# A chunked RWKV-6 recurrence with a SiLU feed-forward: first weight loads moved in the DMA queue, the first two units' values multiplied straight into the rows of x, and first keys moved between engines

## The chip, the cores and the metric

The kernel runs on one core of one Trainium2 chip. The metric is the time of one execution on the device in microseconds (us). The profile is taken by the hardware profiler on one execution. Engines are named as in the profile: PE is TensorE (matrix multiply), PEld its weight load, DVE is VectorE, ACT is ScalarE, POOL is GpSimd, SP is SyncE, which here only issues DMA transfers, one after another in the order in which they are written.

## The reference

The kernel computes a recurrence over 768 tokens for 4 sequences and 8 heads of 48 channels, lays its output out as rows of 384 channels, and sends 3072 such rows through a feed-forward layer with a SiLU.

```python
# r, k, v, w: (4, 8, 768, 48); u: (8, 48)
for t in range(S):
    cur = np.einsum('bhd,bhe->bhde', u[None] * kt, vt)
    y[:, :, t] = np.einsum('bhd,bhde->bhe', rt, state + cur)
    state = wt[:, :, :, None] * state + np.einsum('bhd,bhe->bhde', kt, vt)
x = y.transpose(0, 2, 1, 3).reshape(B * S, H * D)      # 3072 x 384
h = x @ w_in                                            # 384 x 2048
g = h * (1.0 / (1.0 + np.exp(-h)))
return g @ w_out                                        # 2048 x 384
```

Everything is float32.

## The kernel before

**Units.** The work is cut into 12 units, numbered 0 to 11. A unit is 128 tokens of two sequences (b = 0, 1), so 256 rows of x. Two units cover a stretch of 128 tokens, and there are six stretches.

**The recurrence of a unit.** Instead of a loop over tokens the kernel makes a 128 x 128 matrix of scores for each sequence and head, in seven levels (block sizes 1, 2, 4 ... 64). `turn` brings r, k and w into a layout with channels on partitions (`tr`, `tk`, `tw`): for units 0 and 1 by matmuls with the identity (`turn_in`, `turn_out`), for later ones by a DVE transpose. `start_keys`, `grow_keys` and `grow_queries` multiply the keys and queries by products of w (`product`) level by level, `odd_keys` and `odd_ones` copy half of the keys on ACT, `scores` multiplies queries by keys on PE and copies the result into `score` under a mask on DVE. `bonus`, `bonus_sum`, `bonus_spread` and `bonus_write` make the diagonal, the term with u. For units 2 and 3 its numbers go through four small DMAs (`diag`) and five small ACT copies. `turn_apart` and `turn_k` bring the keys back for `update`, which makes the new state.

**From scores to x.** In units 0 and 1 the state is zero, so the output is scores times values. `y` (L872) does that for two heads at a time, in 64 partitions each with 48 used, and copies it to `yt` on ACT. `dense_x` (L910) multiplies `yt` by a 0/1 matrix `dense`, built at the start by `clear_dense` and `make_dense`, which packs the 8 x 48 channels into 3 x 128 partitions, and copies the result to `xt`. From unit 2 on, `y_state` and `y_values` make `yt` and `move_x` (L920) packs it into `xt` by ten DMAs on SP.

**Feed-forward.** `up(i, m)` (L995) multiplies 256 columns of w_in by `xt` (two blocks of 128 hidden channels, each over three blocks of 128 channels of x: 12 PE instructions) and applies the SiLU on ACT. `down` (unit 0) or `quarter` (seven products per unit on sums and differences, `sums` and `weight_sums` on DVE) multiplies by w_out.

**Weights.** Each of 16 blocks of weights (0 to 7 of w_in, 8 to 15 of w_out, 768 KB each) is loaded, split on ACT (`head_weight`, two instructions; `tail_weight`, one, into a PSUM room `p_w` of which there is one), joined on DVE (`join_weight`, two instructions) and added on POOL (`add_weight`). A block's load goes to one of seven places, and `join_weight(i)` issues the load of the block that takes over its place: 6 after 0, 7 after 1, 8 after 2, 9 after 3, 10 after 4, 11 after 5, 12 after 8, 13 after 9, 14 after 10, 15 after 11.

**Order.** Nothing is scheduled by a planner. The order of each engine's instructions is the order in which the steps are written in the `do(...)` lines (L1107 to L1163), and from unit 3 on the order that `mix(i)` gives. All of SP's transfers go through one queue: the blocks of r, k and w of a coming unit (`load_blocks`, 16 transfers for each of the three, of 32 and 16 KB), values (`load_values`, 5), tokens for the diagonal (`load_rk`), weights, diagonal, x and the outputs. A transfer that stands behind another is issued after it, even when what it needs is ready. The blocks of units 2, 3 and 4 are handed out by `block_loads` along the `do` lines; `mix(3)` hands out w and k of unit 5 (8 calls of 4 transfers each, with the values of unit 4 among them), and from `mix(4)` on also r of the next unit. `clear(0)` and `clear(1)` zero the unused half groups of `raw` on ACT once the first two units have been turned.

The line that decides which blocks `mix(i)` loads, in L981, and the steps it hands them to, L985:

```python
loads = [*at(i >= NPAIR and ahead, *block_loads(i + 1, "r")), *at(i + NSLOT < len(units), *block_loads(i + NSLOT, "wk"))]
behind = groups[10 if i < NPAIR else 5 if i == NPAIR else 2:][:4 if i + NSLOT >= len(units) else None]
```

NPAIR is 4 and NSLOT is 2. `move_x(i - 1)` stands in the second group of `mix(i)`, so after all that `mix(i - 1)` loads.

## Time and profile before

| | us |
|---|---|
| three runs | 598.10, 598.62, 599.99 |
| median | 598.62 |
| profiled execution, whole | 599.11 |
| its span, first to last instruction | 597.3 |
| PE busy in the span | 587.5 |
| POOL busy in the key products of L645, all units | 93.9 |
| six weight loads of w_in by SP, median from issue to landing | 7.6 |
| ten moves of x per unit, median from issue to landing of one | 1.9 |

The granted clock of PE is 1.000 throughout. In a timeline row the first number is the start in us from the start of the span, the second the duration, then engine, line, operation, what is written and what is read, and how many instructions the row merges; the brackets give the idle time of that engine just before and what ended it. In rows of SP's queue the duration of one transfer is its issue, not its movement.

### The profile page before, as it was taken

Reading aid. Unit: us, or ns where it says so; the run is one execution under the profiler, and the core shown is the slowest. Engines: PE = TensorE matmul, PEld = TensorE weight load, DVE = VectorE, ACT = ScalarE, POOL = GpSimd, SP = SyncE. Lnnn points to the kernel's source line nnn. Section 1 sums busy time; section 2 is a strip of 40 time slices with the busy share of each in tenths; the row PEclk is TensorE's granted clock in tenths of the full one; section 3 lists DMA queues with packets and bytes.
Section 4 is the critical chain, followed back from the end, with each engine's and each line's share of the span. In section 5 each row is a group of like instructions: output and inputs, shape, how many; then the busy total and the mean of one; then the engine's idle time right before and its main releaser. Section 6 shows DMA issues by size and latency. Waiting matters only on the chain.

```text
span 597.3 us, 14760 instructions
## 1 busy us (share of the span) xinstructions
PE 587.5 (98%) x5790; PEld 527.8 (88%) x5790; DVE 411.6 (69%) x709; ACT 232.7 (39%) x516; POOL 351.5 (59%) x414
## 2 busy tenths in 40 slices
PE   8999999999999999999999999999999999999997
PEld 7787866699899899899899899889889889889997
DVE  7879788798596695596696696686587587542041
ACT  6788874531530540440350351361351251250110
POOL 5998768447578568278378477477477567500000
PEclk9999999999999999999999999999999999999999
DMA  9965794443542543543543643643543531101000
GB/s 227 301 148 149 157 283 75 59 76 51 126 61 66 106 66 52 129 69 53 130 67 55 138 62 52 130 65 52 120 75 52 113 63 27 36 1 28 28 0 27
DMA packets 203078, 53.42 MB, mean 89 GB/s; under 512 B 186752, under 2 KB 194816, under 8 KB 203008
## 3 DMA queue, kind: packets, MB, share of 16 engines
q1 hardware_dynamic: 201424, 51.88, 42.7%
q8 instruction: 46, 0.75, 0.6%
q10 hardware_dynamic: 1584, 0.59, 0.5%
q14 instruction: 24, 0.20, 0.1%
HBM read 43.21 MB, written 5.24 MB: 81 GB/s over the span
## 4 chain that ended last, share of the span: by engine, by line
PE 82%; DVE 5%; POOL 4%; ACT 2%; SPq 2%; DMA 2%; issue 2%; POOLq 0%; DVEq 0%; ACTq 0%
PE p_h L1000 35%; PE p_o L1066 34%; PE p_m L1022 3%; PE p_m L864 2%; PE p_sc L703 2%; PE p_m L843 2%; SPq L123 2%; PE p_m L703 1%; DVE score L721 1%; POOL w_out_sb L255 1%; PE p_sc L892 1%; PE p_sc L819 1%; DMA own<-in_moe_w_out_dram 1%; DMA raw<-in_r_dram 1%; DVE score L604 1%
## 5 line engine op out<-in xcount | busy, mean ns | idle before, releaser
L1000 PE MATMUL p_h<-xt,w_in_sb 128*128 128x256 f32 x1152 | 259.8, 383 | 1.6 <-POOL tk L669 0.7
L1000 PEld LDWEIGHTS p_h<-xt,w_in_sb 128*128 128x128 f32 x1152 | 215.5, 190 | 33.3 <-ACT gt L1009 1.3
L1009 ACT ACTIVATE gt<-p_h 128x512 f32<-128x512 f32 x90 | 53.5, 595 | 172.5 <-PE p_h L1000 172.2
L645 POOL TENSOR_TENSOR tk<-tk,tw 128x256 f32<-128x256 f32 x128 | 93.9, 755 | 35.4 <-issue 21.0
L507 POOL TENSOR_TENSOR ruk<-tokens_rk 128x768 f32<-128x768 f32 (+1 forms) x32 | 51.4, 1616 | 64.4 <-DMA tokens_rk<-in_k_dram 34.6
L1066 PE MATMUL p_o<-own,temps 128*128 128x192 f32 x528 | 87.9, 326 | 0.0
L1066 PE MATMUL p_o<-w_out_sb,gt 128*128 128x192 f32 x508 | 86.4, 326 | 0.0
L1066 PEld LDWEIGHTS p_o<-own,temps 128*128 128x128 f32 x528 | 86.1, 190 | 0.1
L1066 PEld LDWEIGHTS p_o<-w_out_sb,gt 128*128 128x128 f32 x508 | 83.4, 190 | 0.6
L1048 DVE TENSOR_TENSOR temps<-gt 128x256 f32<-128x256 f32 x84 | 50.3, 599 | 25.7 <-ACT gt L1009 25.3
L627 DVE TENSOR_TENSOR tr<-tr,tw 128x512 f32<-128x512 f32 x61 | 54.1, 887 | 14.7 <-PE p_m L703 11.2
L422 POOL TENSOR_TENSOR tw<-tw 128x256 f32<-128x256 f32 (+6 forms) x83 | 40.4, 487 | 35.4 <-DVE tw L374 31.5
L615 ACT COPY tk<-tk 128x256 f32<-128x256 f32 x52 | 21.0, 403 | 102.6 <-POOL tk L645 80.1
L721 DVE COPY_PREDICATED score<-mask,p_sc 128x512 f32<-128x512 int8 x42 | 31.1, 796 | 3.2 <-PE p_sc L703 3.0
L1075 DVE TENSOR_TENSOR partial<-p_o,partial 128x192 f32<-128x192 f32 x33 | 11.7, 355 | 27.8 <-PE p_o L1066 27.8
L1066 PE MATMUL p_o<-w_out_sb,temps 128*128 128x192 f32 x176 | 30.4, 326 | 0.0
L1048 DVE TENSOR_TENSOR temps<-temps,gt 128x256 f32<-128x256 f32 x43 | 29.1, 677 | 1.5
L1075 DVE TENSOR_TENSOR temps<-p_o,partial 128x192 f32<-128x192 f32 x22 | 7.9, 358 | 31.5 <-PE p_o L1066 25.3
L541 DVE TENSOR_REDUCE block_sums<-ruk 128x4 f32<-128x192 f32 (+1 forms) x48 | 24.2, 545 | 7.1 <-POOL ruk L507 7.1
L1066 PEld LDWEIGHTS p_o<-w_out_sb,temps 128*128 128x128 f32 x176 | 28.9, 190 | 0.0
L869 ACT COPY yt<-p_m 48x512 f32<-48x512 f32 x40 | 23.2, 581 | 13.9 <-PE p_m L864 13.1
L703 PEld LDWEIGHTS p_sc<-tr,tk 48*64 48x64 f32 x960 | 17.3, 134 | 12.1 <-issue 7.7
(188 smaller groups left out, 814.2 us busy)
## 6 DMA issues: line engine op xcount, KB each, us to landing
w_out_sb<-in_moe_w_in_dram SPq DMA_DIRECT2D x6, 768.0 KB, 7.6
w_out_sb<-in_moe_w_out_dram SPq DMA_DIRECT2D x4, 768.0 KB, 6.4
own<-in_moe_w_out_dram SPq DMA_DIRECT2D x4, 768.0 KB, 6.1
tokens_rk<-in_r_dram SPq DMA_DIRECT2D x8, 384.0 KB, 4.5
tokens_rk<-in_k_dram SPq DMA_DIRECT2D x8, 384.0 KB, 5.4
tokens_w<-in_w_dram SPq DMA_DIRECT2D x8, 384.0 KB, 6.4
xt<-yt SPq DMA_DIRECT2D x60, 48.0 KB, 1.9
raw<-in_w_dram SPq DMA_DIRECT2D x80, 32.0 KB, 2.2
```

Source lines behind the costliest of these rows:

```text
L422: engine.tensor_tensor(out=up, in0=t[:, :, 0::2], in1=t[:, :, 1::2], op=ALU.mult)
L507: mul = lambda out, one, two: nc.gpsimd.tensor_tensor(out=out, in0=one, in1=two, op=ALU.mult)
L541: add = lambda out, have: nc.vector.tensor_reduce(out=out, in_=have, axis=mybir.AxisListType.X, op=ALU.add)
L627: nc.vector.tensor_tensor(out=odd, in0=odd, in1=tw[i][l][:, :, 0::2][:, :, :, None].to_broadcast([128, Q, L >> (l + 1), c]), op=ALU.mult)
L645: nc.gpsimd.tensor_tensor(out=out, in0=have, in1=odd_products(i, l, b, *blocks), op=ALU.mult)
L703: nc.tensor.matmul(to, lhsT=tk[i][rows, X[l % 2] + p, x * 64:(x + 1) * 64], rhs=have, start=True, stop=True)
L721: nc.vector.copy_predicated(out=dst, mask=masks[l][:, :, None].to_broadcast([128, NB, NP, ni, c]), data=sc[e].rearrange("p (b q) (i c) -> ...
L869: nc.scalar.copy(out=yt[i][PD * e:PD * e + D, x::2, :, :], in_=p_yt[i, e][PD * x:PD * x + D].rearrange("p (q b) t -> p q b t", b=NB))
L1000: nc.tensor.matmul(p_h[:, a, :], lhsT=w_in_sb[:, c, f * 128:(f + 1) * 128], rhs=xt[i][:, c, :], start=(c == 0), stop=(c == KC - 1))
L1009: nc.scalar.activation(out=gt[i, m], in_=p_h, func=AF.Silu)
L1048: nc.vector.tensor_tensor(out=out, in0=one, in1=two, op=op)
L1066: nc.tensor.matmul(p, lhsT=left(f), rhs=right[:, f, :], start=(f == 0), stop=(f == FH - 1))
```

## The change

- `y` and `dense_x` are replaced by `x_products` and `x_copy` for units 0 and 1. For each block of 128 channels of x and each half of it, one matmul of 64 columns with the later of the two heads' scores, then one of 48, 32 or 16 columns with the earlier head's scores, which overwrites the rows that belong to that head. `dense`, `clear_dense` and `make_dense` go, and so do the copies to `yt`.
- `turn_apart` comes ahead of the products of both units.
- `clear(0)` and `clear(1)` on ACT go; `clear_rest` clears the last 240 columns of each part of `raw` on POOL at the start.
- Unit 1's `start_keys` runs on DVE instead of POOL, and unit 1's key turns come earlier.
- In unit 2, `odd_ones` and the first `start_keys` come earlier, the values' load, the shuffle `reverse_v` and `weight_sums(0)` later.
- On SP, blocks 8 to 11 of unit 2 (r) come behind weight 11; values of unit 2 and tokens of unit 3 come behind weights 14 and 15; unit 3's blocks come behind those; r of unit 4 moves into `mix(3)`.
- The five copies of the diagonal's numbers of unit 3 go from ACT to DVE.

```diff
-    def clear(i):
-        clear_all(raw[:, i % NSLOT].rearrange("p x b h d -> p (x b h d)").rearrange("p (g d) -> p g d", d=32)[:, :, D - 32:32])
+    def clear_rest():
+        for i in range(NSLOT):
+            nc.gpsimd.memset(raw[:, i].rearrange("p x b h d -> p x (b h d)")[:, :, H * 2 * D + PD - D:], 0.0)
...
-        nc.scalar.copy(out=both_b[:, 0], in_=diag[i][0])
+        copy = nc.vector.tensor_copy if i > NTOK else nc.scalar.copy
+        copy(out=both_b[:, 0], in_=diag[i][0])
         for g in range(4):
-            nc.scalar.copy(out=both_b[(3 - g) * 32:(4 - g) * 32, 1], in_=diag[i][1][g * 32:(g + 1) * 32])
+            copy(out=both_b[(3 - g) * 32:(4 - g) * 32, 1], in_=diag[i][1][g * 32:(g + 1) * 32])
...
+    def x_products(i, b):
+        if b == 0:
+            xt[i] = pt.tile([128, KC, TU], F32, name="xt", bufs=1)
+        to = p_x[i, b] = ps.tile([128, KC, L], F32, name="p_h", bufs=2) if i == 0 else bank("p_m", KC, L)
+        have = whole[i][b]
+        places = []
+        for c in range(KC):
+            for row in range(0, 128, PD):
+                at = c * 128 + row
+                last = (at + PD - 1) // D
+                assert at // D == last - 1
+                places += [(c, row, last, PD), (c, row, last - 1, last * D - at)]
+        places.sort(key=lambda place: -place[3])
+        for c, row, h, columns in places:
+            at = c * 128 + row
+            nc.tensor.matmul(to[row:row + columns, c, :], lhsT=have[:, at:at + columns],
+                             rhs=score[:, i % NSC, h % 2, b * NP + h // 2, :], start=True, stop=True)
+
+    def x_copy(i, b):
+        (nc.vector.tensor_copy if (i, b) == (0, 1) else nc.scalar.copy)(out=xt[i][:, :, b * L:(b + 1) * L], in_=p_x[i, b])
...
-        loads = [*at(i >= NPAIR and ahead, *block_loads(i + 1, "r")), ...
+        loads = [*at(i >= NPAIR - 1 and ahead, *block_loads(i + 1, "r")), ...
...
-       (bonus_sum, 0, 0), (clear_dense,), (clear_state,), ...
+       (bonus_sum, 0, 0), (clear_state,), (clear_rest,), ...
-       (make_dense,), (beat, 16))
+       (beat, 16))
...
-    do((bonus, 1, 0), (bonus, 1, 1), (bonus, 1, 2), *both(y, 0), (turn_apart, 0), (join_weight, 0), (add_weight,),
-       (product, 1, 0), (tail_weight, 1), (turn, 1, 0, "k"), (join_weight, 1), (dense_x, 0, 0), (turn, 1, 1, "k"),
-       (dense_x, 0, 1), (grow_queries, 1, 0), (odd_ones, 1), (tail_weight, 2), (turn_k, 0), (head_weight, 2),
-       (start_keys, 1, nc.gpsimd, True), (add_weight,), (up, 0, 0), (join_weight, 2), *blocks[4:8],
-       (start_keys, 1, nc.gpsimd, False), (add_weight,), (tail_weight, 3), (odd_keys, 1, 1), (head_weight, 3), (grow_keys, 1, 1),
+    do((bonus, 1, 0), (bonus, 1, 1), (product, 1, 0), (bonus, 1, 2), (turn_apart, 0), *both(x_products, 0), (join_weight, 0), (add_weight,),
+       *both(turn, 1, "k"), (grow_queries, 1, 0), (start_keys, 1, nc.vector, True), *both(x_copy, 0), (tail_weight, 1), (odd_ones, 1), (turn_k, 0),
+       (join_weight, 1), (add_weight,), (start_keys, 1, nc.vector, False), (tail_weight, 2), (odd_keys, 1, 1), (head_weight, 2), (up, 0, 0),
+       (join_weight, 2), *blocks[4:8], (grow_keys, 1, 1), (add_weight,), (tail_weight, 3), (head_weight, 3),
...
-    others = {1: [(bonus_sum, 1, 0), (bonus_sum, 1, 1), (load_rk, 2), *blocks[8:12]], 2: [*both(update, 0)],
-              3: [(bonus_spread, 1), (reverse_v, 1), (clear, 1), (load_values, 2)]}
+    others = {1: [(bonus_sum, 1, 0), (bonus_sum, 1, 1), (load_rk, 2)], 2: [*both(update, 0), *blocks[8:10]],
+              3: [(bonus_spread, 1), (reverse_v, 1), *blocks[10:12]]}
...
-... (up, 0, 7), *both(y, 1), (turn_apart, 1),
-       (tail_weight, 9), (turn_k, 1), (dense_x, 1, 0), (head_weight, 9, [0]), (dense_x, 1, 1), (head_weight, 9, [1]),
-       (join_weight, 9), (add_weight,), (tail_weight, 10), (head_weight, 10), *both(update, 1), (bonus_sum, 2, 1), (load_rk, 3), (up, 1, 0), *both(turn, 2, "w"))
+... (up, 0, 7), (turn_apart, 1), *both(x_products, 1),
+       (turn_k, 1), *both(x_copy, 1), (tail_weight, 9), (head_weight, 9),
+       (join_weight, 9), (add_weight,), (tail_weight, 10), (head_weight, 10), *both(update, 1), (bonus_sum, 2, 1), (up, 1, 0), *both(turn, 2, "w"))
     blocks = block_loads(3)
-    others = {0: [(up, 1, 1), (down, 0, 0, 0), *both(turn, 2, "k"), (product, 2, 0), (product, 2, 1)],
-              1: [(up, 1, 2), *both(turn, 2, "r"), *[(product, 2, l) for l in range(2, NL)], *blocks[0:3]],
-              2: [(down, 0, 0, 1), (odd_ones, 2), (start_keys, 2, nc.gpsimd, True), (grow_queries, 2, 0), *blocks[3:6]],
-              3: [(up, 1, 3), (start_keys, 2, nc.gpsimd, False), (reverse_v, 2), *blocks[6:9]], 4: [(level, 2, 1), (up, 1, 4), *blocks[9:12]],
-              5: [(down, 0, 0, 2), (up, 1, 5), (weight_sums, 0)]}
+    others = {0: [(up, 1, 1), (down, 0, 0, 0), *both(turn, 2, "k"), (odd_ones, 2), (product, 2, 0), (product, 2, 1)],
+              1: [(up, 1, 2), *both(turn, 2, "r"), (start_keys, 2, nc.gpsimd, True), *[(product, 2, l) for l in range(2, NL)], (load_values, 2)],
+              2: [(down, 0, 0, 1), (grow_queries, 2, 0), (load_rk, 3), *blocks[0:2]],
+              3: [(up, 1, 3), (start_keys, 2, nc.gpsimd, False), *blocks[2:5]], 4: [(level, 2, 1), (up, 1, 4), *blocks[5:8]],
+              5: [(down, 0, 0, 2), (up, 1, 5), *blocks[8:12]]}
...
-    blocks = block_loads(4)
-    do(*blocks[0:2], ..., (down, 0, 1, 1), (sums, 1, 0))
-    do(blocks[2], ..., (prepare, 2, 5), (down, 0, 1, 2),
+    blocks = block_loads(4, "wk")
+    do(*blocks[0:2], ..., (down, 0, 1, 1), (sums, 1, 0), (weight_sums, 0))
+    do(blocks[2], ..., (prepare, 2, 5), (reverse_v, 2), (down, 0, 1, 2),
```

## The prediction

> **What bounds the kernel now.** I read the page's busy shares, the waits in the PE timeline, then the SyncE queue's timeline, since most of the change moves issues on it. TensorE (PE) first:
>
> ```profile
> PE 587.5 (98%) x5790; PEld 527.8 (88%) x5790; DVE 411.6 (69%) x709; ACT 232.7 (39%) x516; POOL 351.5 (59%) x414
> ...
> 35.90 2.83 PE L1000 MATMUL p_h<-xt,w_in_sb 128*128 128x256 f32 x12 [0.74 <-POOL tk L669]
> 66.40 1.09 PE L878 MATMUL p_m<-score,vt 128*64 128x128 f32 x16
> 67.32 1.04 PE L878 MATMUL p_m<-score,vq 128*64 128x128 f32 x16
> 68.92 2.94 PE L916 MATMUL p_m<-yt,ruk 128*128 128x128 f32 x24
> 83.11 1.45 PE L1022 MATMUL p_m<-w_out_sb,own 128*128 128x384 f32 x4
> 89.92 0.70 PE L703 MATMUL p_sc<-tr,tk 48*64 48x64 f32 x32 [1.48 <-POOL tk L669]
> 158.03 8.39 PE L1000 MATMUL p_h<-xt,w_in_sb 128*128 128x256 f32 x36 [0.63 <-ACT gt L1009]
> 192.51 13.22 PE L1000 MATMUL p_h<-xt,w_in_sb 128*128 128x256 f32 x60
> ```
>
> From about 90 us PE works without a gap, apart from the 0.63 at 158. So what moves PE at 90 or later moves the end one for one, unless a later wait takes it back. Between 30 and 66 us PE shows few gaps, yet VectorE (DVE) sets the pace there: from 42.27 to 67.5 its rows follow one another with no wait over 0.15 us. Now SyncE's queue:
>
> ```profile
> 71.42 0.39 SPq L206 DMA_DIRECT2D own<-in_moe_w_out_dram  x1
> 84.58 1.08 SPq L206 DMA_DIRECT2D own<-in_moe_w_out_dram  x2
> 142.72 9.22 SPq L123 DMA_DIRECT2D raw<-in_r_dram  x16
> 153.01 2.45 SPq L467 DMA_DIRECT2D diag<-own_sums  x4
> 158.96 11.30 SPq L123 DMA_DIRECT2D raw<-in_w_dram  x16
> 173.90 7.84 SPq L123 DMA_DIRECT2D raw<-in_k_dram  x16
> 181.85 6.35 SPq L928 DMA_DIRECT2D xt<-yt  x10
> 199.81 11.19 SPq L123 DMA_DIRECT2D raw<-in_r_dram  x16
> ```
>
> The queue has almost no idle time from 142.72 to 188.20, and the ten moves of unit 3's x (`xt<-yt`) stand at its tail. Their last issue starts near 187.6; the tile view of xt gives a median of 1.9 us from issue to landing, so x is whole at 189.5. `up(3, 0)` starts at 192.51 and meets x's last third after four of its twelve matmuls (2.79/12 each), at 193.4. The cover is 3.9 us. Unit 4 shows what happens when the cover is gone: x issued from 231.55 to 237.83, `up(4, 0)` at 238.29, and its twelve matmuls take 3.01 instead of 2.86.
>
> **The change part by part.**
>
> *Start-up.* ScalarE (ACT) loses `make_dense` (2.10 at 12.75) and `clear(0)` (1.47 at 15.94). Both are followed by a copy that waits for POOL (0.78 and 0.17), so nothing. POOL swaps one memset (0.74 for 768 numbers) for two of 720; its 3.72 us wait up to 13.72 hides them.
>
> *Values straight into x, unit 0.* Per unit, 32 instructions at L878 (1.96 us) and 24 at L916 (2.94) become 48 narrower ones. An L878 instruction takes 61 ns, an L916 one 122; the new ones are 64 columns or fewer, as L878's, so 48 x 61 = 2.94 (upper end 5.9): PE saves 1.96. Which engine gets it? After the last score copy (29.64) PE turns the keys back to 30.4 and ends the products at 33.3. ACT: four key copies 30.5 to 31.75, first x copy to 32.45, the second weight's tail to 33.3. DVE: join of weight 0 to 31.7, queries to 32.4, the two `start_keys` it takes over (four in 1.32) to 33.05, second x copy after PE to 34.0, join of weight 1 to 35.95 (35.03 now). ACT then does tail 2 (0.87), an odd-key copy (0.35), head 2 (1.86) and a Silu (0.5), so tail 3 starts at 39.6; in the row it starts at 39.43. From there to 66.4 DVE's order is unchanged and full. POOL sheds 2.6 us of keys but adds weight 2 about 1 us later (join 2, then the grown keys); `up(0, 2)` then ends at 45.0, before ACT asks for it at 46.0. Gain 0 (ends -0.4 and +0.4).
>
> *Values into x, unit 1.* From 66.40 to `up(1, 0)` at 72.65 are 6.25 us. They become 0.63 (keys back), 2.94 (products) and 0.9 (state update), with the second x copy just inside: `up(1, 0)` at 70.85, 1.8 earlier.
>
> *Weights first in the queue.* Weight 11's load no longer stands behind 16 blocks of r (issue 71.42 to about 60); 14 and 15 issue when their joins free the place, about 79 and 82, instead of 84.58. ACT's waits for those loads (0.65, 1.34, 1.56) go. But tail 9 now stands behind both x copies, at 70.5 instead of 68.89. Following DVE from there with the durations of the rows (join 9, state copies 1.12, sums 1.01, turns 1.29, join 10, turns, join 11), join 11 ends at 82.0 (81.76 now) and POOL's add ends at 84.15 (83.73). PE needs weight 11 in the second half of the matmuls that start at 83.11 now, so they start at 84.25 against 84.39: of the 1.8 us only 0.15 survives. What is late next is that add.
>
> *Third unit's first keys sooner.* POOL now does them right after add 11, ending at 85.5 instead of 89.87, so PE's 1.48 us gap at 89.92 closes: 1.6 ahead at 90. Weights 12 to 15 are added 1 to 4 us earlier than now and are not waited for. `weight_sums(0)` (1.75) and the shuffle of v (0.59) move on DVE to 106 and 112; by the rows the masked copies there keep 0.1 to 0.5 us before PE's next burst. I take -1.4 at 145 us (ends 0, if the gap reopens under another wait, and -3.3, if the 1.8 survives too).
>
> *Unit 3's loads.* Values and tokens now stand ahead of its blocks, which start about 4.5 us later (near 90), land near 119 and are read at 128 to 131. x of unit 2 follows in the same queue: landing about 144.6, needed at about 145.2. Thin cover; if it fails PE waits up to 2 us at `up(2, 0)`, but that lies before the next wait and does not add to it.
>
> *Unit 3's diagonal.* Five small copies go from ACT (0.20 and 0.84, waiting for the diag DMAs to 156.64) to DVE, which now idles 2.06 there. The two Silus held up at 157.39 go sooner and PE's 0.63 (and 0.08 at 163.56) closes. The diag issues, at 153.01 behind r, can follow the sums at 152.3: 0.7 sooner.
>
> *r of unit 4, from 142.72 to behind unit 3's diagonal.* `mix(3)` now issues 16 + 16 + 5 + 16 transfers where it issued 37, all ahead of `move_x(3)`. The 16 take 16 x 0.49 = 7.85 at best (7.84 at 173.90), 9.22 at 142.72, 11.19 at 199.81 behind big token loads. Those loads still come just ahead, but their wait only moves from w to r, so I take 8.2, near the first two. x of unit 3 then lands 8.2 - 0.7 - 1.4 = 6.1 later, at 195.6, against a need at 193.4 now: PE resumes 2.2 us *later* than before, and PE's own 2.1 us lead (1.4 + 0.7) is waited away. Later units have the same queue in the same order; the queue's wait for the block sums (192.33 to 195.20) absorbs its lateness, so nothing adds up and nothing is won back.
>
> The Trainium skill, "DMA: Bandwidth & Descriptors", Rules for kernel authors, speaks against this step: it says to issue a DMA early and wait late, and that transfers under 64 KB are mostly overhead. Its fit (2.0 us plus bytes over 436 GB/s, in the section on the anatomy of one DMA, for another issuing engine) would make 16 transfers of 16 and 32 KB in series some 33 us, an estimate, and the kernel about 27 us slower; the rows show 0.49 each because they overlap, and the sum goes by the rows.
>
> **Sum.** +2.2 on the profiled execution of 599.11 (span 597.3 and 1.8 around it) is 601.3. The median shown, 598.62, lies 0.5 below that execution, so the forecast is 600.8.
>
> **The rivals.**
> - *The queue keeps up* (ends faster). If x of unit 3 landed by about 191.3, PE would keep its lead: 598.62 - 2.1 = 596.5. That needs the 16 transfers to cost under 3.9 us, half of the cheapest row. For it: r no longer stands before the diag. Against: no row of 16 block transfers is under 7.8.
> - *No lead arrives.* Join 11 or another wait takes the 1.4 as well. The queue's clock starts from the sums of unit 3, which follow PE's burst at 144.6, so the loss is 8.2 - 0.7 - 3.9 = 3.6: 602.2. Against it: POOL has 4 us in hand for the keys.
> - *The lead is larger and cancels.* With -3.3 at 145, +0.3: 598.9. For it: weights 14 and 15 come well ahead; against: add 11.
> - *More than one x is late*, unit 2's or a later one's too, or r takes 11.19: 604.
>
> **How the numbers follow.** Chances: forecast 0.45, queue keeps up 0.15, no lead 0.17, cancels 0.18, more than one 0.05. About 0.3% (1.8 us) is what a measurement of this kernel tells from no change: faster is under 596.8, slower over 600.4. The forecast's own range, 599.4 to 602.2 (r from 7.85 to 9.22, lead from 0.9 to 2.0), lies about three quarters above 600.4: 0.34 slower, 0.11 same. Slower 0.34 + 0.17 + 0.05 = 0.56, same 0.11 + 0.18 = 0.29, faster 0.15. The range must hold cancels, forecast and no lead: 596.9 to 603.0; it leaves out the queue that keeps up and the last rival.
>
> **What the changed profile would show.** Right: no wait at the keys' burst near 88; r's 16 issues near 157 and x of unit 3 issued from about 188 instead of 181.85; PE waiting 3 to 5 us on `xt` inside the first `up` after 190, the largest gap of the run; no 0.63 gap at 158. Wrong: `up(3, 0)` before 191 with x landed; a wait on the add of weight 11 over 3 us; PE waiting near 36 to 60; the products at 120 ns each. What would overturn the forecast is a queue that issues block transfers faster than any row here shows, or a lead at 145 us beyond 4 us.

## The result, and the profile after

| | before | after |
|---|---|---|
| median of four runs, us | 599.31 (598.10 to 600.73) | 606.33 (606.01 to 606.51) |
| ratio, 95% interval | | 1.0113 (1.0093 to 1.0134) |
| profiled execution, us | 599.11 | 606.51 |
| its span, us | 597.3 | 604.7 |

The changed kernel is 1.1% slower. The forecast of 600.8 had the sign right and the size wrong: 606.33 lies 3.3 us above the end of the range. In the experiments below, three executions that lie far above the rest of their runs (675.17, 1005.42 and 1603.56 us) enter no ratio. The page of the changed kernel:

```profile
PE 588.2 (97%) x5774; PEld 525.4 (87%) x5774; DVE 413.1 (68%) x718; ACT 225.3 (37%) x495; POOL 350.9 (58%) x411
PEclk9999999999999799999999999999999999999999
L983 PE MATMUL p_h<-xt,w_in_sb 128*128 128x256 f32 x1152 | 263.1, 386 | 7.8 <-DMA xt<-yt 3.9
```

Two things are new. PE waited 3.9 us for `xt<-yt`, the moves of x. And the row of the granted clock has a 7 in the slice from 196.5 to 211.6 us, where the kernel before had only nines. PE's timeline shows where the rest lies (start, duration, engine, line, operation, tiles, shapes, count, idle time before). Here and below only the rows that matter are shown:

```profile
35.59 2.83 PE L983 MATMUL p_h<-xt,w_in_sb 128*128 128x256 f32 x12 [1.59 <-DVE xt L875]
43.98 2.86 PE L983 MATMUL p_h<-xt,w_in_sb 128*128 128x256 f32 x12 [1.78 <-POOL w_in_sb L255]
66.25 2.86 PE L983 MATMUL p_h<-xt,w_in_sb 128*128 128x256 f32 x12 [0.15 <-POOL w_in_sb L255]
69.67 1.66 PE L871 MATMUL p_m<-score,vt 128*64 128x128 f32 x24
71.25 1.66 PE L871 MATMUL p_m<-score,vq 128*64 128x128 f32 x24
73.69 5.45 PE L983 MATMUL p_h<-xt,w_in_sb 128*128 128x256 f32 x24
86.97 1.56 PE L1005 MATMUL p_m<-w_out_sb,gt 128*128 128x384 f32 x4 [1.37 <-POOL w_out_sb L255]
91.05 0.70 PE L684 MATMUL p_sc<-tr,tk 48*64 48x64 f32 x32
158.46 8.43 PE L983 MATMUL p_h<-xt,w_in_sb 128*128 128x256 f32 x36
192.98 0.70 PE L983 MATMUL p_h<-xt,w_in_sb 128*128 128x256 f32 x2
196.08 0.67 PE L983 MATMUL p_h<-xt,w_in_sb 128*128 128x256 f32 x2 [2.40 <-DMA xt<-yt]
198.25 15.00 PE L983 MATMUL p_h<-xt,w_in_sb 128*128 128x256 f32 x56 [1.50 <-DMA xt<-yt]
213.18 0.69 PE L684 MATMUL p_sc<-tr,tk 48*64 48x64 f32 x32
```

Set against the rows of before, PE is this much later (a minus is earlier):

| place | before | after | later by |
|---|---|---|---|
| `up(0, 7)` done | 66.40 | 69.04 | 2.64 |
| `up(1, 0)` | 72.65 | 73.69 | 1.04 |
| keys' burst near 90 | 89.92 | 91.05 | 1.13 |
| `up` after the burst at 158 | 158.03 | 158.46 | 0.43 |
| `up(3, 0)`, first matmul | 192.51 | 192.98 | 0.47 |
| its last third (x whole) | 193.4 | 198.25 | 4.85 |
| next burst | 205.66 | 213.18 | 7.52 |
| span | 597.3 | 604.7 | 7.4 |

So the loss is made at three places: 2.6 us by 69 us (of which unit 1's products and closed gaps, less the new wait for weight 11, win 2.2 back by 158), 4.4 around the waits for x (3.9 of it idle), and 2.7 right behind them, where PE had work and was slow. The last is the clock, in the view of busy time by stretch (length of the stretch, then busy time and instructions of PE, PEld, DVE, ACT and POOL, granted clock, DMA share, GB/s):

```profile
190.00:196.90 6.90, 4.35 (x81) 3.28 (x79) 4.62 (x8) 0.00 (x0) 4.62 (x4) 1.00 0.23 54
196.90:203.80 6.90, 5.55 (x13) 4.50 (x14) 1.73 (x4) 0.89 (x2) 0.74 (x2) 0.51 0.62 137
203.80:213.00 9.20, 9.20 (x44) 7.98 (x42) 3.07 (x4) 3.70 (x10) 6.83 (x6) 1.00 0.66 127
```

The granted clock is 0.51 over the 6.9 us that begin with the second wait. The trace's own record of the clock gives 0.5 for 6.83 us from 196.85. SyncE's queue explains the wait:

```profile
81.54 3.51 SPq L206 DMA_DIRECT2D own<-in_moe_w_out_dram  x2
...
91.41 8.22 SPq L123 DMA_DIRECT2D raw<-in_w_dram  x16
...
152.95 3.08 SPq L447 DMA_DIRECT2D diag<-own_sums  x4
...
159.54 10.27 SPq L123 DMA_DIRECT2D raw<-in_r_dram  x16
169.86 3.91 SPq L123 DMA_DIRECT2D raw<-in_w_dram  x8
...
181.73 7.84 SPq L123 DMA_DIRECT2D raw<-in_k_dram  x16
189.69 7.02 SPq L911 DMA_DIRECT2D xt<-yt  x10
```

Weights 14 and 15 are issued at 81.54. Unit 3's blocks start at 91.41 (85.71 before), the diagonal at 152.95 (153.01), r of unit 4 behind it, and x of unit 3 at 189.69 (181.85).

### The profile page after: what moved, and what is told of

It reads as the page before. It is cut to its first block, busy times and chain, and to the rows that moved or that the text cites. A ratio compares the mean times of both kernels' runs of the same rounds, so it can differ in the third digit from the quotient of the medians.

```text
span 604.7 us, 14708 instructions
## 1 busy us (share of the span) xinstructions
PE 588.2 (97%) x5774; PEld 525.4 (87%) x5774; DVE 413.1 (68%) x718; ACT 225.3 (37%) x495; POOL 350.9 (58%) x411
## 4 chain that ended last, share of the span: by engine, by line
PE 79%; SPq 6%; DMA 4%; DVE 4%; POOL 3%; ACT 2%; issue 2%; POOLq 0%; DVEq 0%; ACTq 0%
PE p_h L983 36%; PE p_o L1049 30%; SPq L123 4%; PE p_m L1005 3%; PE p_sc L684 2%; PE p_m L845 2%; DMA u_bc<-in_u_dram 2%; POOL tk L626 2%; PE p_m L824 2%; DMA w_out_sb<-in_moe_w_out_dram 1%; PE p_m L684 1%; SPq L911 1%; DVE tk L650 1%; PE p_sc L885 1%; PE p_sc L800 1%
## 5 line engine op out<-in xcount | busy, mean ns | idle before, releaser
L983 PE MATMUL p_h<-xt,w_in_sb 128*128 128x256 f32 x1152 | 263.1, 386 | 7.8 <-DMA xt<-yt 3.9
L626 POOL TENSOR_TENSOR tk<-tk,tw 128x256 f32<-128x256 f32 x128 | 93.2, 749 | 47.6 <-issue 28.5
L1031 DVE TENSOR_TENSOR temps<-gt 128x256 f32<-128x256 f32 x84 | 47.8, 569 | 28.2 <-ACT gt L992 27.9
L608 DVE TENSOR_TENSOR tr<-tr,tw 128x512 f32<-128x512 f32 x61 | 55.4, 908 | 14.0 <-PE p_m L684 10.9
L635 POOL TENSOR_TENSOR tk<-tk,tw 128x256 f32<-128x256 f32 x32 | 28.0, 894 | 0.0
```

The lines of the kernel that those rows point to most:

```text
L608: nc.vector.tensor_tensor(out=odd, in0=odd, in1=tw[i][l][:, :, 0::2][:, :, :, None].to_broadcast([128, Q, L >> (l + 1), c]), op=ALU.mult)
L626: nc.gpsimd.tensor_tensor(out=out, in0=have, in1=odd_products(i, l, b, *blocks), op=ALU.mult)
L635: nc.gpsimd.tensor_tensor(out=have, in0=have, in1=odd_products(i, l, b, [2, NP * ni]), op=ALU.mult)
L983: nc.tensor.matmul(p_h[:, a, :], lhsT=w_in_sb[:, c, f * 128:(f + 1) * 128], rhs=xt[i][:, c, :], start=(c == 0), stop=(c == KC - 1))
L1031: nc.vector.tensor_tensor(out=out, in0=one, in1=two, op=op)
```

## The experiments

The kernel before had medians from 597.89 to 599.58 us beside these runs, a difference larger than some of the effects. So each run is given as a ratio to the kernel before as it ran beside it, with its 95% interval.

### Is r of unit 4 alone to blame?

Two runs: the changed kernel with r loaded early again, and the kernel before with only r loaded late.

```diff
-        loads = [*at(i >= NPAIR - 1 and ahead, *block_loads(i + 1, "r")), ...
+        loads = [*at(i >= NPAIR and ahead, *block_loads(i + 1, "r")), ...
...
-    blocks = block_loads(4, "wk")
+    blocks = block_loads(4)
```

> The changed kernel with r of unit 4 loaded where the kernel before loads it. Queue theory (r behind the diagonal makes x of unit 3 late, PE's waits of 2.40 and 1.50 us follow from that, and the halved clock of 6.83 us follows from the waits): no wait on xt near 196, granted clock 1.000 throughout, and 606.3 - 3.9 - 3.1 = 599.3 us, at most 599.8, that is the kernel before within 0.3%. Rival one (x is late for another reason, the later blocks of unit 3 or the values ahead of them): the waits stay, over 603 us. Rival two (the clock falls for its own reason, not after the wait): no wait but a clock under 1, about 602.4 us. Under all of them PE's lateness of about 1.1 us near 91 us stays.

Measured: 604.78 us, 1.0102 (1.0079 to 1.0126). There is no wait for x, but the time hardly moves. PE, SyncE, DVE and ACT:

```profile
158.64 5.45 PE L983 MATMUL p_h<-xt,w_in_sb 128*128 128x256 f32 x24
167.53 5.49 PE L983 MATMUL p_h<-xt,w_in_sb 128*128 128x256 f32 x12 [3.44 <-ACT gt L992]
...
147.19 7.84 SPq L123 DMA_DIRECT2D raw<-in_r_dram  x16
...
157.08 2.45 SPq L447 DMA_DIRECT2D diag<-own_sums  x4
...
159.50 0.17 DVE L576 COPY both_b<-diag 128x16 f32<-128x16 f32 x1 [2.69 <-DMA diag<-own_sums]
...
163.10 2.24 ACT L781 COPY score<-p_sc 32x128 f32<-32x128 f32 x8 [4.85 <-DVE score L585]
```

The wait has moved. r now starts at 147.19 (142.72 in the kernel before) and the diagonal's transfers go at 157.08 instead of 153.01. DVE's copies of the diagonal's numbers wait for them, ACT's score copies wait for DVE's masked write behind those (4.85 us), two Silus stand behind the score copies, and PE waits 3.44 us for the PSUM buffers that the Silus empty. The clock halves again, for 6.83 us from 166.75. The halved clock is not all of it: the traced execution is the slowest of four (605.80), and one with a granted clock of 1.000 still took 602.85. The queue theory as I had stated it falls: putting r back does not help.

The second, with the same lines the other way round in the kernel before:

> The kernel before with one edit: r of unit 4 moved behind unit 3's diagonal. Queue theory: x of unit 3 lands 8.2 - 0.7 = 7.5 us later against a cover of 3.9, so PE waits about 3.6 us on xt, the clock halves after it for about 6.8 us and costs about 3.1 more: 599.3 + 6.7 = 606.0 us (604.5 to 607). If the clock halves only together with other parts of the change: 602.9 us with a clock of 1.000. If the move is harmless by itself: 599.3 us.

Measured: 604.59 us, 1.0103 (1.0082 to 1.0124), waits on x of 1.59 and 1.49 us:

```profile
192.95 0.67 PE L1000 MATMUL p_h<-xt,w_in_sb 128*128 128x256 f32 x2 [1.59 <-DMA xt<-yt]
195.11 14.01 PE L1000 MATMUL p_h<-xt,w_in_sb 128*128 128x256 f32 x56 [1.49 <-DMA xt<-yt]
```

So the move of r costs as much by itself as the whole change, as forecast for this run. Its four executions hint at the price of the clock: the one with a granted clock of 0.997 (one halved stretch of 3.41 us, from 195.43) took 602.36 us, the three with 0.994 took 604.48 to 605.10. A second stretch of 3.41 us at half clock can cost 1.7 at most, so their waits must have differed too.

### What makes the queue late

The changed kernel with every load back in its old place (r of unit 2 ahead of weight 11, values and tokens ahead of weights 14 and 15, r of unit 4 early by the edit above):

```diff
-    others = {1: [..., (load_rk, 2)], 2: [*both(update, 0), *blocks[8:10]],
-              3: [(bonus_spread, 1), (reverse_v, 1), *blocks[10:12]]}
+    others = {1: [..., (load_rk, 2), *blocks[8:12]], 2: [*both(update, 0)],
+              3: [(bonus_spread, 1), (reverse_v, 1), (load_values, 2)]}
...
-... (bonus_sum, 2, 1), (up, 1, 0), ...
+... (bonus_sum, 2, 1), (load_rk, 3), (up, 1, 0), ...
...
-              1: [..., (load_values, 2)],
-              2: [..., (load_rk, 3), *blocks[0:2]],
-              3: [..., *blocks[2:5]], 4: [..., *blocks[5:8]],
-              5: [..., *blocks[8:12]]}
+              1: [..., *blocks[0:3]],
+              2: [..., *blocks[3:6]],
+              3: [..., *blocks[6:9]], 4: [..., *blocks[9:12]],
+              5: [...]}
```

> The changed kernel with every load in the place where the kernel before has it: r, values and tokens ahead of weights 11, 14 and 15 as before, unit 3's blocks right behind, r of unit 4 early. New theory of the queue (moving the values and tokens behind weights 14 and 15 leaves SyncE idle while it waits for those weights and makes it some 4.5 us late at 143 us; that lateness is paid either at unit 3's diagonal, when r of unit 4 goes first, or at unit 3's x, when it goes last, and each wait halves the clock): no wait over 1 us after 90 us, clock 1.000 after 90 us, and the time of the kernel before plus 0.5 to 1.4 us. Rival (the five diagonal copies on VectorE hold up the Silus whatever the queue does): a wait of 2 to 4 us near 160 to 168 us stays, and the time is 5 us or more over the kernel before.

Measured: 600.74 us, 1.0015 (0.9993 to 1.0038), clock 0.999, and the largest wait after 90 us is this one:

```profile
164.85 2.86 PE L983 MATMUL p_h<-xt,w_in_sb 128*128 128x256 f32 x12 [0.30 <-ACT gt L992]
```

Its blocks of unit 3 start at 85.69. The rival (diagonal copies on DVE hold up the Silus whatever the queue does) falls as an account of this loss. No run puts these copies back on ACT beside a late queue, so whether they make its price there larger is not shown. Together the runs make a square:

| | r of unit 4 early | r of unit 4 late |
|---|---|---|
| loads as before | 1.0015 (changed kernel otherwise) | 1.0103 (kernel before otherwise) |
| weights first | 1.0102 (changed kernel otherwise) | 1.0113 (the changed kernel) |

Either edit alone costs 1%, and both cost little more than one. Weights first makes the queue 4.5 us late at r of unit 4 (147.19 against 142.72) and 5.7 us at unit 3's blocks, since weights 14 and 15 can't be issued before their places are free (81.54) and 6.2 us of values and tokens now stand behind them, where they used to fill that time. With r early that lateness falls on the diagonal; with r late the queue catches up ahead of the diagonal and pays at x.

### The clock behind the wait

The changed kernel with transposes that nothing reads ahead of unit 3's feed-forward, so that PE does not idle while x is late:

```diff
     def up(i, m):
+        if (i, m) == (3, 0):
+            p_f = ps.tile([128, 2, TU], F32, name="p_h", bufs=2)
+            for x in range(36):
+                nc.tensor.transpose(p_f[:, 0, 0:L], ident, ident)
```

> The changed kernel with 36 transposes that nothing reads (about 4.4 us) on PE ahead of the first matmuls of unit 3's feed-forward, in the time in which PE waits for x. If the halved clock follows from PE's idling: the same late x, no wait over 0.5 us there, clock 1.000, and 606.3 - 3.1 + 0.1 = 603.3 us. If the clock falls for another reason: clock 0.994 and 606.4 us. The output is the same, the added work is thrown away.

Measured: 604.43 us (604.18 to 604.94), 1.0081 (1.0053 to 1.0109), clock 1.000.

```profile
193.14 4.15 PE L982 MATMUL p_h<-ident 128*128 128x128 f32 x36
197.12 1.03 PE L987 MATMUL p_h<-xt,w_in_sb 128*128 128x256 f32 x4
198.91 12.32 PE L987 MATMUL p_h<-xt,w_in_sb 128*128 128x256 f32 x56 [0.75 <-DMA xt<-yt]
```

The same 56 matmuls take 12.32 us here and 15.00 in the changed kernel: the halved clock costs 2.68 us. That agrees with the record: of the 6.83 us PE worked 5.43 (198.25 to 203.68), and half of that is 2.7. They also start 0.66 later (198.91 against 198.25; the first move of x is issued at 190.16 here, 0.47 later), so 2.0 of it shows in the span, 602.7 against 604.7. That PE's idling brings the halved clock is shown: x is at least as late and only the idling is gone.

### The loss before 69 us

First the engine alone. In the changed kernel two of DVE's four rows of unit 1's first keys are long; DVE, then POOL, then ACT:

```profile
32.66 2.32 DVE L650 TENSOR_TENSOR tk<-tk,tw 128x128 f32<-128x128 f32 x2
...
37.21 2.32 DVE L650 TENSOR_TENSOR tk<-tk,tw 128x128 f32<-128x128 f32 x2
...
32.22 2.21 POOL L255 TENSOR_TENSOR w_in_sb<-temps 128x768 uint32<-128x768 uint32 x1 [0.44 <-DVE temps L243]
37.38 1.91 POOL L255 TENSOR_TENSOR w_in_sb<-temps 128x768 uint32<-128x768 uint32 x1 [2.95 <-DVE temps L243]
...
37.33 0.88 ACT L231 ACTIVATE p_w<-w_out_sb 128x768 f32<-128x768 uint16 x1 [2.28 <-DVE temps L243]
39.57 0.43 ACT L596 COPY tk<-tk 128x256 f32<-128x256 f32 x1 [1.36 <-DVE tk L650]
...
42.22 0.85 ACT L231 ACTIVATE p_w<-w_out_sb 128x768 f32<-128x768 uint16 x1
```

Each pair takes 2.32 us where four such rows at the kernel's start take 1.31. The long row of each pair (2.02 us) starts while a weight add runs on POOL and ends 0.25 us behind it. ACT waits 2.28 and then 1.36 us, and the tail of weight 3 is at 42.22 (39.43 before). The edit puts the keys back on POOL in the new order:

```diff
-       ... (start_keys, 1, nc.vector, True), ...
+       ... (start_keys, 1, nc.gpsimd, True), ...
-       ... (start_keys, 1, nc.vector, False), ...
+       ... (start_keys, 1, nc.gpsimd, False), ...
```

> The changed kernel with unit 1's first keys (start_keys) on POOL, as in the kernel before, in their new places. Port theory (two of the four DVE rows took 2.02 us instead of 0.39 because POOL's weight adds ran beside them, which pushed the joins of weights 2 and later back): no DVE row of start_keys after 30 us, joins 2 and 3 about 2 to 3 us earlier, up(0, 7) ends 2.2 us earlier, the third unit's x still waits: 606.3 - 2.2 = 604.1 us (603.5 to 605.2; the upper end if the 2.7 us of keys on POOL delay its weight adds). Rival (the new order of tails, heads and weight loads delays the pipeline, whoever makes the keys): 606.3 within 0.5 us, PE's lateness at 69 us as in the changed kernel.

Measured: 606.61 us, 1.0140 (1.0121 to 1.0159). PE starts `up(0, 0)` 1.1 us earlier and has lost it by the third `up`:

```profile
39.39 0.42 ACT L596 COPY tk<-tk 128x256 f32<-128x256 f32 x1 [2.29 <-POOL tk L650]
...
41.86 1.82 POOL L255 TENSOR_TENSOR w_in_sb<-temps 128x768 uint32<-128x768 uint32 x1
...
43.73 2.86 PE L983 MATMUL p_h<-xt,w_in_sb 128*128 128x256 f32 x12 [2.72 <-POOL w_in_sb L255]
```

The rival holds: the copy of the odd keys stands ahead of the head of weight 2 on ACT and now waits 2.29 us for POOL, and POOL adds weight 2 only after the grown keys. With r early as well:

> Both edits on the changed kernel: r of unit 4 early again, and unit 1's first keys on POOL. If the two causes are separate they add up: 599.3 to 599.8 less 2.2 = 597.1 to 597.6 us, 0.3% faster than the kernel before. If PE's lead near 90 us is waited away at unit 3's diagonal or x: 599 to 600 us. If the keys on POOL only move the wait to the weight adds: 599 us.

Measured: 606.38 us, 1.0126 (1.0103 to 1.0148), so none of the three outcomes: PE waits 2.73 us for weight 2 at 44 us and 3.84 us at unit 3's diagonal, and the 2.73 us halved the clock there too, which the same wait of 2.72 in the run before did not.

Then the order of steps, with keys on POOL and the products into x kept:

```diff
-    do((bonus, 1, 0), (bonus, 1, 1), (product, 1, 0), (bonus, 1, 2), (turn_apart, 0), *both(x_products, 0), (join_weight, 0), (add_weight,),
-       *both(turn, 1, "k"), (grow_queries, 1, 0), (start_keys, 1, nc.vector, True), *both(x_copy, 0), (tail_weight, 1), (odd_ones, 1), (turn_k, 0),
-       (join_weight, 1), (add_weight,), (start_keys, 1, nc.vector, False), (tail_weight, 2), (odd_keys, 1, 1), (head_weight, 2), (up, 0, 0),
-       (join_weight, 2), *blocks[4:8], (grow_keys, 1, 1), (add_weight,), (tail_weight, 3), (head_weight, 3),
+    do((bonus, 1, 0), (bonus, 1, 1), (bonus, 1, 2), *both(x_products, 0), (turn_apart, 0), (join_weight, 0), (add_weight,),
+       (product, 1, 0), (tail_weight, 1), (turn, 1, 0, "k"), (join_weight, 1), (x_copy, 0, 0), (turn, 1, 1, "k"),
+       (x_copy, 0, 1), (grow_queries, 1, 0), (odd_ones, 1), (tail_weight, 2), (turn_k, 0), (head_weight, 2),
+       (start_keys, 1, nc.gpsimd, True), (add_weight,), (up, 0, 0), (join_weight, 2), *blocks[4:8],
+       (start_keys, 1, nc.gpsimd, False), (add_weight,), (tail_weight, 3), (odd_keys, 1, 1), (head_weight, 3), (grow_keys, 1, 1),
```

> The changed kernel with the steps between the two first units in the order of the kernel before (head of weight 2 ahead of the odd keys on ScalarE, second half of the keys and the add of weight 2 ahead of the grown keys on POOL, keys on POOL), the products into x kept. Order theory (the odd keys ahead of head 2, and join 1 behind copies and keys, made weights 2 and 3 late): no wait of PE on weight 2 near 43 us, up(0, 7) ends 2.2 to 2.6 us earlier, the wait of 1.4 us on weight 11 shrinks or stays, and, with the wait for x of unit 3 as it is, 603.7 to 604.3 us. Rival (the products into x or the cleared tile's room cause it): PE is as late at 69 us as in the changed kernel, 606.3 us.

Measured: 604.31 us, 1.0078 (1.0050 to 1.0105). The wait near 43 us is gone, `up(0, 7)` starts at 64.94 instead of 66.25, the diagonal's transfers go 1.3 us earlier and x of unit 3 1.4 us earlier, so the gain arrives at the end. It would be larger, but in this trace the clock halves for 3.41 us after a wait of 1.64 that ends at 35.50.

Kernels whose first 16 us are the same differ by up to 1.2 us there (15.52 to 16.71 at the mark below), so the stretch is best measured from PE's own mark, its burst of scores behind the wait of 0.6 us near 16 us, to the start of `up(0, 7)`:

| kernel | mark | `up(0, 7)` | between |
|---|---|---|---|
| before | 15.65 | 63.61 | 47.96 |
| changed | 16.10 | 66.25 | 50.15 |
| keys on POOL, new order | 15.81 | 65.99 | 50.18 |
| keys on POOL, old order (clock halved from 35.9) | 15.94 | 64.94 | 49.00 |
| the same, x copies sooner (three versions below) | 16.66, 16.02, 15.52 | 64.65, 64.00, 63.49 | 47.99, 47.98, 47.97 |

The change cost 2.2 us here. In the new order the engine of the keys makes no difference. The old order, with the keys on POOL, gives 1.15 of the 2.2 back, although the wait at 35 us now halves the clock; with the x copies sooner that wait goes, and all of the 2.2 is back. What the engine costs in the old order is tried on the version with the tail of weight 9 first (below):

```diff
-       (start_keys, 1, nc.gpsimd, True), ...
+       (start_keys, 1, nc.vector, True), ...
-       (start_keys, 1, nc.gpsimd, False), ...
+       (start_keys, 1, nc.vector, False), ...
```

> The run with the tail of weight 9 first, with one edit: unit 1's first keys on VectorE instead of POOL, in the old order of steps. Port theory (a VectorE product with both inputs in SBUF waits while POOL adds weights): one or two of the four rows take 1.5 to 2 us instead of 0.39, join 2 starts 1.5 to 3 us later than with the keys on POOL, PE is 1 to 2.5 us later at 66 us, and the time is 1 to 2.5 us over that run, 599.5 to 601 us. Rival (in the changed kernel the rows were long only because of its order of steps): 0.39 us each, and 598.4 us or less, POOL being 2.7 us freer.

Measured: 598.28 us, 0.9995 (0.9978 to 1.0012), the same as that version with the keys on POOL. DVE:

```profile
35.94 2.07 DVE L608 TENSOR_TENSOR tr<-tr,tw 128x512 f32<-128x512 f32 x1
37.94 0.69 DVE L650 TENSOR_TENSOR tk<-tk,tw 128x128 f32<-128x128 f32 x2
...
40.48 2.33 DVE L650 TENSOR_TENSOR tk<-tk,tw 128x128 f32<-128x128 f32 x2
```

The long rows are there in this order too, and one falls on the queries (2.07 instead of 0.69). From mark to `up(0, 7)` it takes 49.81 against 48.99, 0.8 us more, but the time of the whole kernel doesn't show it. Each of the two traces has one halved stretch of 3.41 us in this part, from 48.18 here and from 35.69 there, behind different waits. The port theory is right about the rows and wrong about their price.

### The products alone, and the wait for weight 11

The kernel before with `y` and `dense_x` replaced by `x_products` and `x_copy`, in their old places:

```diff
-... *both(y, 0), (turn_apart, 0), ... (dense_x, 0, 0), ... (dense_x, 0, 1), ...
+... *both(x_products, 0), (turn_apart, 0), ... (x_copy, 0, 0), ... (x_copy, 0, 1), ...
-... *both(y, 1), (turn_apart, 1), ... (dense_x, 1, 0), ... (dense_x, 1, 1), ...
+... *both(x_products, 1), (turn_apart, 1), ... (x_copy, 1, 0), ... (x_copy, 1, 1), ...
```

> The kernel before with one edit: the values multiplied straight into the rows of x in units 0 and 1, all else in its old order. Theory of the prediction (PE saves 1.6 us in unit 1, but the add of weight 11 and then the third unit's first keys hold PE where they held it): up(1, 0) 1.5 us earlier than in the kernel before, a wait for weight 11 or a longer wait than 1.48 us at 90 us, and the time of the kernel before within 0.3%. Rival (the saving survives): 1.3 us or more faster. Rival (48 narrow products cost more than they save): slower by 1 us.

Measured: 599.60 us, 1.0024 (1.0003 to 1.0046): no gain, if anything a loss. PE does the work sooner and then idles, and the idling costs clock:

```profile
35.34 4.47 PE L1002 MATMUL p_h<-xt,w_in_sb 128*128 128x256 f32 x12 [1.65 <-DVE xt L894]
...
72.73 0.56 PE L904 MATMUL p_m<-vt,kq 128*48 128x48 f32 x16 [1.33 <-ACT xt L894]
...
73.92 7.11 PE L1002 MATMUL p_h<-xt,w_in_sb 128*128 128x256 f32 x24 [0.26 <-ACT xt L894]
```

Twelve matmuls take 4.47 us instead of 2.83, and 24 take 7.11 instead of 5.45: 1.65 lost at each place. In the kernel before, the matmuls of `dense_x` (the 2.94 us at 68.92, for one) stood between the products and `up`, where PE now waits for the copies to `xt`.

With loads and order of steps both as before, what is left of the change is the products, unit 2's first keys sooner, two moved DVE steps and the diagonal's copies on DVE:

> Both: loads where the kernel before has them, and the steps between the first units in its order. What is left of the change is the products into x, the third unit's first keys sooner, the shuffle and weight sums later, and the diagonal copies on VectorE. If queue and order explain all of the loss: faster than the kernel before by 1.5 to 2.5 us (the 1.48 us gap at 90 us and the 0.63 at 158 closed). If add of weight 11 still holds PE: the time of the kernel before within 0.3%.

Measured: 599.43 us, 1.0004 (0.9983 to 1.0026), with the wait for weight 11 still at 1.35 us. Unit 3's diagonal is thin here too, with r of unit 4 ahead of it:

```profile
72.78 0.96 DVE L242 SCALAR_TENSOR_TENSOR p_w<-w_out_sb,p_w 128x768 uint32<-128x768 uint32 x1 [3.61 <-ACT p_w L231]
...
165.99 2.86 PE L983 MATMUL p_h<-xt,w_in_sb 128*128 128x256 f32 x12 [2.45 <-ACT gt L992]
```

The wait of 2.45 us did not halve the clock. Join 9 starts at 72.78 on DVE, since the tail of weight 9 stands behind both x copies on ACT. Hence:

```diff
-       (turn_k, 1), *both(x_copy, 1), (tail_weight, 9), (head_weight, 9),
+       (turn_k, 1), (tail_weight, 9), *both(x_copy, 1), (head_weight, 9),
```

> As the run with loads and first steps in the old order, and the tail of weight 9 ahead of unit 1's x copies on ScalarE. Theory (the tail of weight 9 behind both x copies made joins 9 to 11 and the add of weight 11 late): join 9 starts near 70 us instead of 72.78, PE's wait of 1.35 us for weight 11 near 85 us closes or falls under 0.5, and the time is 1 to 1.5 us under that run, 598 us. Rival (POOL's products of w ahead of the add decide): the wait stays within 0.3 us, 599.4 us.

Measured: 598.40 us, 0.9995 (0.9980 to 1.0010):

```profile
70.21 0.97 DVE L242 SCALAR_TENSOR_TENSOR p_w<-w_out_sb,p_w 128x768 uint32<-128x768 uint32 x1 [0.80 <-ACT p_w L231]
```

Join 9 starts at 70.21, the wait for weight 11 is gone, and PE is at 88.17 at the keys' burst (89.92 before). The place of that tail was the cause of the wait.

### Versions to beat both

Three versions add to this the x copies of unit 0 both on ACT, ahead of unit 1's key copies. The first and third also split r of unit 4 (12 transfers early, 4 late); the second and third load unit 3's tokens behind weight 14 instead of ahead of it.

```diff
-       (product, 1, 0), (tail_weight, 1), (turn, 1, 0, "k"), (join_weight, 1), (x_copy, 0, 0), (turn, 1, 1, "k"),
-       (x_copy, 0, 1), (grow_queries, 1, 0), ...
+       (product, 1, 0), (tail_weight, 1), *both(x_copy, 0), *both(turn, 1, "k"), (join_weight, 1),
+       (grow_queries, 1, 0), ...
...
+        loads = [*at(i >= NPAIR - 1 and ahead, *block_loads(i + 1, "r")[0 if i >= NPAIR else 3:]), ...
```

> A version to beat both: as the run before it, with both x copies of unit 0 on ScalarE ahead of the second unit's key copies, and r of unit 4 split, 12 transfers in the old place and 4 behind unit 3's diagonal. If the waits near 35 us (1.64), near 85 us (1.35) and near 160 to 166 us (0.3 to 2.5) all come from these: no wait over 0.8 us after 30 us, clock 1.000, x of unit 3 about 2 us later than its old time and still in time, and 1.5 to 3 us under the kernel before. If the four late transfers already make x late: a wait on xt near 193 us and 600 us or more.

> A second version to beat both: products into x with both x copies of unit 0 on ScalarE, the old order between the units, tail of weight 9 ahead of unit 1's x copies, all loads where the kernel before has them but for the tokens of unit 3, which come behind the load of weight 14 instead of ahead of it. If the wait near 35 us (1.65 with a halved clock) goes by the copies and the one near 98 us (1.55) by the earlier load of weight 14: no wait over 0.8 us after 34 us, clock 1.000, and 1 to 2 us (0.2 to 0.3%) under the kernel before. If run to run differences of the start (about 1 us) hide it: the kernel before within 0.3%.

> The second version once more, for its trace: most of its executions had a granted clock of 0.997 and were some 3 us longer, and the traced one had not. If the thin place is unit 3's diagonal (r of unit 4 ahead of it in SyncE's queue): the trace shows PE waiting 1.5 to 3.5 us near 160 to 168 us and a halved clock after it. If it is weight 14 or 15: a wait near 85 to 100 us. If it is x of unit 3: a wait near 190 us.

> The first version to beat both (r of unit 4 split, 12 transfers ahead of unit 3's diagonal and 4 behind it) with the tokens of unit 3 behind the load of weight 14, as in the second. If the diagonal is the thin place, the split keeps it in time in every execution: clock 1.000, no wait near 98 us, 1 to 2.5 us under the kernel before. If the tokens' place makes the second version slow: clock 0.997 in most executions here too, and 600 us.

Measured: the first 597.96 us, 0.9990 (0.9970 to 1.0011), clock 1.000 in all ten executions; the second 600.17, 1.0027 (1.0007 to 1.0048), and once more 599.24, 1.0006 (0.9984 to 1.0029), clock 0.997 in many executions; the third 597.65, 0.9976 (0.9950 to 1.0002). Sooner x copies close the wait at 35 us in all three. The trace of this repeat shows the thin place of the second version:

```profile
162.88 4.54 PE L983 MATMUL p_h<-xt,w_in_sb 128*128 128x256 f32 x12 [2.35 <-ACT gt L992]
```

It is unit 3's diagonal again, and the wait there halves the clock (12 matmuls in 4.54 us instead of 2.86). In the first trace of the same kernel that wait was 0.29 us. The third version is the best, but its interval still touches 1: no version is shown to beat the kernel before.

## Why the prediction was wrong

Two steps failed. The lead of 1.4 us that PE was to have at 145 us did not come, because the new order of steps in unit 0, put at a gain of 0, cost 2.2 us. And the clock behind PE's wait, 2.68 us, was put at nothing.

**r of unit 4 behind the diagonal: right, and its price too.** From the first diagonal transfer to the first move of x it took 28.84 us before and 36.74 after, 7.9 us more; the step had 8.2. r itself took 10.27, but the w blocks that no longer stand behind the token loads took 7.8 instead of 11.30. The signs came nearly as written: r's 16 issues from 159.54 (said: near 157), x from 189.69 (188), the largest wait of the run on `xt` inside the first `up` after 190, 3.9 us in the stated 3 to 5. That this wait has the forecast size says nothing for the lead: a lead that does not come moves PE and x alike.

**"I take -1.4 at 145 us": failed.** PE was 1.13 later instead, a miss of 2.5 us. The rival *no lead arrives* names what followed: the diagonal's issue, meant to come 2.1 earlier by lead and closed gap, came 0.06 earlier, and x with it. x's last third was ready at 198.25 where the sum had 195.6; 2.05 of the difference is the diagonal, 0.67 the ten moves themselves (7.02 against 6.35), r gave 0.3 back, and 0.2 stays unaccounted for.

**"Gain 0 (ends -0.4 and +0.4)" in unit 0 is where the lead went.** The products were as forecast (1.58 us from start to start for 24 instructions, 66 ns each, for 61). But the step put the four `start_keys` on DVE at 1.32, where they took 4.64, and the tail of weight 3 came at 42.22 for a forecast of 39.6. The runs show that the order around those rows sets PE's pace (with the keys on POOL in the same order it is as slow, 50.18 against 50.15): ACT's head of weight 2 behind the odd keys, and POOL's add of weight 2 behind the grown keys. My working listed ACT's steps in the new order (tail 2, odd-key copy, head 2), but end to end, without the 2.28 and 1.36 us of waits that this order brings. The 2.2 us lost from mark to `up(0, 7)` are nearly the whole miss of 2.5. A stated sign of being wrong, PE waiting near 36 to 60, came as well: 1.78 us at 43.98 and 0.83 at 48.17.

**The halved clock was not in the sum at all.** It cost 2.68 us, shown by the busy PE, as much as the lost lead. The trace of before gave no warning: its clock is 1.000 throughout and its longest wait after 2 us is 1.48.

**Right.** Unit 1's products: 4.65 us from `up(0, 7)` to `up(1, 0)` for 6.25, 1.6 for a forecast 1.8. Weight 11's add as "late next" (PE waited 1.37 us for it), with the tail of weight 9 behind the x copies as its cause. The 1.48 at 89.92 and the 0.63 at 158 closed. Unit 3's blocks about 4.5 us later (5.7), with `up(2, 0)` not held up.

**The sum anew,** in spans: x ready 4.85 later where 2.2 was forecast, and 2.68 of clock, are 7.5; the span grew by 7.4. The start-up's 0.45 us is within what kernels with the same start differ by at the mark. The forecast's inner range of 599.4 to 602.2 does not quite follow from its ends (r 7.85 with a lead of 2.0 gives 599.9, r 9.22 with 0.9 gives 602.3); nothing turns on it.

A reading that the rows of before would have allowed: DVE's products with both inputs in SBUF show their price there. The group of L627 by form, with the least, the median and the greatest duration in ns, in the kernel before, says it:

```profile
L627 DVE TENSOR_TENSOR tr<-tr,tw x61: 667/692/2293, 12.3 to 526.2; 128x512 f32<-128x512 f32 x61
```

All 23 of these rows that took over 0.9 us started while a POOL instruction ran; those that started up to 0.28 us ahead of one kept 0.67 to 0.69. So the rows of before give a price from both ends. The Trainium skill, "SBUF — State Buffer", section "Who interferes with whom", says of this that a VectorE instruction with two SBUF inputs contends with a GpSimd one that reads SBUF, and that the later of the two waits. The long rows agree with it; their cost to the whole kernel did not show in its time.

## What to carry to other kernels

A queue that issues in order has one lateness, and moving a transfer in it only chooses who pays: here 4.5 us made by loads that wait for their places cost 1% at the diagonal or, with r moved behind the diagonal, 1% at x; moving r alone cost 1% at x as well; and with all loads in their old places no cost was measured. When a change makes PE wait 1.5 us or more, price the clock behind the wait as well. Where an engine takes over steps, follow what stands behind them on every engine that waits for them, and not only the durations of the rows.

## What the hardware showed unexpectedly

The granted clock falls to 0.5 for 3.41 us or for 6.83 us, twice that, after PE has idled. The traces of these kernels show such stretches after single waits of 1.64 to 1.67 us (35 us), 2.35, 2.73, 3.44 and 3.84, and after waits close together, as 1.33 and 0.26, 1.59 and 1.49, 2.40 and 1.50. They show none after others of 1.48, 1.55, 1.60, 1.65, 1.78, 2.45 or 2.72. So the length of the wait does not decide alone.

Where the wait lies decides with it. The record of the clock in each trace says when it was first full and when it fell to 0.5. The distance between the two is a whole number of times 3.4133 us in each of the 16 traces, of 17, that have a fall: 191.146 us, 56 times, in the changed kernel, 30.720, 9 times, and 157.013, 46 times, in others. So time can be cut into windows of 3.4133 us from the first full clock on, and PE's idle time summed in each window of full clock. After a window with 2.2 us idle or more the clock was always halved (14 windows), after one with 1.58 to 1.99 sometimes (5 of 13), after one with less never. The wait of 2.73 at 44 us lay in one window. The wait of 2.72 at the same place in the run before was split into 1.26 and 1.46 by the end of a window, and the one of 2.45 into 1.70 and 0.75; neither halved the clock. The clock stayed halved for a second window where PE still idled 0.78 us or more in the first (four traces), and came back where that was 0.13 or less.

A stretch of 3.41 us full of work costs about 1.65 us (12 matmuls, 4.47 for 2.83), and the one of 6.83 us that began within the wait cost 2.68.

The Trainium skill, "TensorE: Matmul & The Clock Gate", section "Part 1: The HAM clock gate", states a free-running window of 3413 ns and a halved clock after at least one idle window of about 3.4 us. The length of the windows and their fixed places agree with it. A whole window of idling was not needed here: 1.58 us within one window was enough in one case and 2.2 or more in every case, and the measurement decides. What tells the cases between 1.58 and 1.99 apart is not known.

What stays open: why the first 16 us differ by up to 1.2 us (over the 17 traces PE's mark is later where the clock is first full later, from 15.52 with 4.26 us to 16.71 with 7.36, a correlation of 0.88 that no run tests), and which executions of the last versions met a halved clock for which wait, since only one of each run is traced.
